# Tiles of three and of two blocks of 128 rows in an expert loop, with part of the small tiles' weight splits on GpSimd

## The chip, the cores and the metric

The kernel runs on one core of a Trainium2 chip. The metric is the device time of one execution in microseconds. Five engines work side by side, each on its own row of instructions: PE (TensorE, matmuls and transposes), DVE (VectorE), ACT (ScalarE), POOL (GpSimd) and SP (SyncE, which here only issues DMAs). An instruction starts when the one before it on its engine has been issued and the semaphores that it waits for are up.

## What is computed

Three stages follow each other on 24576 rows (8 sequences of 3072) of 256 float32 numbers. The first is a filter in the frequency domain along each sequence, the third a feed-forward network on every row. The change is in the second:

```
do_compute = x @ w_skip > 0
e_idx = argmax(x[do_compute] @ w_gate)          # one of 8 experts for each row
h = maximum(xc[mask] @ w1[e], 0.0)              # 256 -> 1024, for the rows of expert e
y[mask] = gate_w[mask, None] * (h @ w2[e])      # 1024 -> 256
out[do_compute] = xc + y
```

With the reference's inputs 12185 rows are computed. They make 13, 13, 13, 11, 12, 14, 11 and 12 blocks of 128 for the eight experts, the last block of each being filled up with padding.

## The kernel before

Every float32 operand of a matmul is split into a high and a low part, and three products are summed (high by high, high by low, low by high), since PE takes the parts at a higher rate. The high part is a copy that rounds, the low part is the operand minus the high part.

The first stage (class `Phase1`) also computes each row's expert and writes, with 192 indirect DMAs of GpSimd (L720), the list `lst` of the rows of each expert. Before the second stage, `Phase2.table` (L892 to L929) makes from the counts a table with one entry for each tile: its expert `te` and its first place in the list `tr`. A tile has TT = 384 places, three blocks of 128, so each expert's rows are rounded up to a multiple of three blocks.

`Phase2.run` (L1094 to L1119) then runs one loop over the table. Its body is a hand-made software pipeline. While tile i goes through both matmuls, the rows of tile i + 1 are gathered and turned, and its weights are loaded and split. In the order of the code one iteration does:

- `rc` is copied from `rn` on DVE (L1095): the rows of this tile, kept for the sum at the end.
- `gather` (L946): after a `hold`, three indirect DMAs of GpSimd bring the next tile's rows into `rn` (L952). A `hold` (L971) is an add of one column on GpSimd. It makes GpSimd wait, so that the DMA behind it needs no wait of its own.
- three adds of one column on GpSimd make sure that the `ob` tiles are free (L1098).
- `fetch` loads the next `w1` (1 MB, SP, L944).
- for each f of 8 slices: `up(f)` has six matmuls of 384 columns (L1018), then `hh` (ACT, L1020) and `hl` (DVE, L1021) empty PSUM. `split2(f)` splits this tile's `w2` into high (ACT, L995) and low (DVE, L996) in `w2x`.
- `tokens` loads the list's entries for a later tile into `pn` (L939), `fetch2` the next `w2` (L974).
- for each of the three blocks j: `down(j)` has eight pairs of matmuls of 512 and 256 columns (L1031, L1034). Behind `down(0)` stands `turn`, the transposes of the next tile's rows on PE (L1003) with `xh` (ACT, L1008) and `xl` (DVE, L1009). `split1` splits the next `w1` in quarters (ACT L989, DVE L990). `finish` (L1043 to L1050) adds the parts of `py` into `sb`, makes `ob` from it, holds, and scatters the rows back with one indirect DMA of GpSimd.

Each engine works through its own row in this order, so what stands later in the code waits for what stands ahead of it on the same engine. At the end of the loop all engines meet at a barrier, and GpSimd executes a drain before it.

Of the kernel before, what the change touches and what calls it, by code (L numbers as in the profile page):

```python
# [20 lines left out]
N1, N2, NT = 96, 32, 24  # L21
KP = 4 * NT + 2
NE, FE, FF = 8, 1024, 2048
TT = 384
CAP = NTOK + TT
BIG = 1 << 20
LAM = 0.01
NTB = 96
HINT = (mybir.EngineType.PE,)
# [37 lines left out]
class Flow:  # L67
# [8 lines left out]
    def __init__(self, bufs):  # L76
        self.bufs, self.steps, self.writers, self.readers = bufs, [], {}, {}
# [79 lines left out]
class Phase1:  # L157
# [385 lines left out]
    def inverse(self, b):  # L543
# [3 lines left out]
        for q in range(8):  # L547
# [16 lines left out]
            for g in (2 * q, 2 * q + 1):  # L564
# [297 lines left out]
class Keep:  # L862


    def __init__(self, nc, pool):
        self.nc = nc
        t = lambda n, shape, dt=F32: pool.tile(shape, dt, tag=n, name=n)
        self.base, self.ident = t("base", [128, NE]), t("ident", [128, 128])
        self.index, self.indexf = t("index", [32, NTB // 32, 1], I32), t("indexf", [32, NTB // 32, 1])
        self.start, self.one = t("start", [32, NE]), t("one", [32, NE])  # L870
        self.pack = t("pack", [32, 2 * NTB // 32, 32])

    def count(self):
# [4 lines left out]
    def consts(self):  # L878
        V = self.nc.vector
        V.tensor_copy(self.indexf, self.index)  # L880
        V.memset(self.one, 1.0)
        V.memset(self.pack, 0.0)
        for e in range(NE):
            V.memset(self.start[:, e : e + 1], float(TT - 1 - (e * CAP - 1 - BIG)))


class Phase2:
# [3 lines left out]

    def table(self, cp):  # L892

        nc, keep = self.nc, self.keep
        V = nc.vector
        NC = NTB // 32

        def tl(shape, tag, dt=F32):
            return cp.tile(shape, dt, tag=tag, name=tag)

        cf, nt, cum, off = (tl([32, NE], "tb" + n) for n in "abcd")
        ni = tl([32, NE], "tbi", I32)
        V.tensor_tensor(cf, keep.base[0:32, :], keep.start, op=ALU.add)
        V.tensor_copy(ni, cf)
        V.tensor_scalar(ni, ni, 7, None, op0=ALU.logical_shift_right)
        V.tensor_copy(nt, ni)
        V.tensor_scalar(nt, nt, float(-(-2048 // (TT // 128))), None, op0=ALU.mult)
        V.tensor_copy(ni, nt)
        V.tensor_scalar(ni, ni, 11, None, op0=ALU.logical_shift_right)
        V.tensor_copy(nt, ni)  # L910
        V.tensor_tensor_scan(cum, keep.one, nt, 0.0, op0=ALU.mult, op1=ALU.add)
        V.tensor_scalar(off, nt, -float(TT), float(CAP), op0=ALU.mult, op1=ALU.add)
        ge = tl([32, NC, NE], "tbg")
        over = lambda v: v.rearrange("p (o e) -> p o e", o=1).to_broadcast([32, NC, NE])
        V.tensor_tensor(ge, keep.indexf.to_broadcast([32, NC, NE]), over(cum), op=ALU.is_ge)
        ef, rf = tl([32, NC, 1], "tbx"), tl([32, NC, 1], "tby")
        V.tensor_reduce(ef, ge, axis=AX.X, op=ALU.add)
        V.tensor_tensor(ge, ge, over(off), op=ALU.mult)
        V.tensor_reduce(rf, ge[:, :, 0 : NE - 1], axis=AX.X, op=ALU.add)
        V.scalar_tensor_tensor(rf, keep.indexf, float(TT), rf, op0=ALU.mult, op1=ALU.add)  # L920
        V.tensor_scalar(keep.pack[:, 0:NC, 0:1], ef, float(NE - 1), None, op0=ALU.min)
        V.tensor_scalar(keep.pack[:, NC : 2 * NC, 0:1], rf, float(NE * CAP - TT), None, op0=ALU.min)
        turned = tl([32, 2 * NC, 32], "tbt")
        V.transpose(out=turned, in_=keep.pack)
        te = tl([1, 2 * NTB], "tbp", I32)
        V.tensor_copy(te, turned[0:1].rearrange("p c i -> p (c i)"))
        self.te, self.tr = te[:, 0:NTB], te[:, NTB : 2 * NTB]
        self.tn = tl([1, 1], "tbn", I32)
        V.tensor_copy(self.tn, cum[0:1, NE - 1 : NE])  # L929

    def reg(self, ap, lo, hi, **kw):
        return self.nc.values_load(
# [3 lines left out]
    def tokens(self, at):  # L936
        nc = self.nc
        r = self.reg(self.tr[0:1, at], 0, NE * CAP - TT, engines=[mybir.EngineType.SP])
        nc.sync.dma_start(self.pn, self.lst[ds(r, TT), :].rearrange("(p j) w -> p j w", p=128))  # L939

    def fetch(self, at):
        nc = self.nc
# [49 lines left out]
    def split2(self, f):  # L992
        nc = self.nc
        hi, lo = self.w2x[:, f, 0:256], self.w2x[:, f, 256:512]
        nc.scalar.activation(hi, self.w2r[:, f, :], AF.Copy)  # L995
        nc.vector.tensor_tensor(lo, self.w2r[:, f, :], hi.bitcast(F32), op=ALU.subtract)  # L996

    def turn(self):
        nc = self.nc
        for h in range(2):  # L1000
# [7 lines left out]
            nc.scalar.activation(self.xh[:, h, :], pt, AF.Copy)  # L1008
            nc.vector.tensor_tensor(self.xl[:, h, :], pt, self.xh[:, h, :].bitcast(F32), op=ALU.subtract)  # L1009

    def up(self, f):
        nc = self.nc
        ph = self.ps.tile([128, TT], F32, tag="ph", name="ph", bufs=4)
        k = 0
        fs = slice(f * 128, f * 128 + 128)
        for h in range(2):
            for w, x in ((self.w1h, self.xh), (self.w1h, self.xl), (self.w1l, self.xh)):
                nc.tensor.matmul(ph, w[:, h, fs], x[:, h, :], start=k == 0, stop=k == 5)  # L1018
                k += 1
        nc.scalar.activation(self.hh[:, f, :], ph, AF.Relu)  # L1020
        nc.vector.scalar_tensor_tensor(  # L1021
            self.hl[:, f, :], ph, 0.0, self.hh[:, f, :].bitcast(F32), op0=ALU.max, op1=ALU.subtract
        )

    def down(self, j):
# [34 lines left out]
    def run(self, ctx):  # L1060
        tc, nc = self.tc, self.nc
# [5 lines left out]
        t = lambda n, shape, dt=F32, pool=cr: pool.tile(shape, dt, tag=n, name=n)  # L1067
# [6 lines left out]
        t = lambda n, shape, dt=F32: cp.tile(shape, dt, tag=n, name=n)  # L1074
# [19 lines left out]
        with tc.For_i(0, n, 1, iteration_sync="reg_based", hint_engines=HINT) as it:  # L1094
            nc.vector.tensor_copy(self.rc, self.rn)  # L1095
            self.gather()
            for o in self.ob:
                nc.gpsimd.tensor_tensor(o[:, 0:1], self.dummy, self.dummy, op=ALU.add)  # L1098
            self.fetch(ds(it + 1, 1))
            for f in range(8):  # L1100
                self.up(f)
                self.split2(f)
                if f == 5:
                    nc.vector.tensor_copy(self.pc, self.pm)
                    nc.vector.tensor_copy(self.pm, self.pn)
            self.tokens(ds(it + 2, 1))
            self.fetch2()
            last = None
            for j in range(self.nj):
                py = self.down(j)  # L1110
                if j == 0:
                    self.turn()
                if last is not None:
                    self.finish(j - 1, last)
                for k in range(4 * j // self.nj, 4 * (j + 1) // self.nj):
                    self.split1(k)
                last = py
            self.finish(self.nj - 1, last)
# [204 lines left out]
```

## Time and profile before

| what | value |
|---|---|
| three runs | 3606.24, 3608.36 (median), 3610.34 us |
| the profiled execution | 3606.89 us |
| its span, first to last instruction | 3605.1 us |
| mean granted clock of PE | 0.983 |
| busy in the span | PE 97%, DVE 65%, ACT 63%, GpSimd 17% |
| the expert loop, first to last `rc` copy | 837.4 to 1448.6 us, 36 tiles |

A row of a timeline gives the start of an instruction, how long it took, its engine, line and operation, and in brackets how long the engine was idle before it and what ended that. In a stretch, the granted clock is that of PE: 1.00 is 2.4 GHz, 0.50 is 1.2 GHz. GpSimd's indirect DMAs are shown with the time in which GpSimd makes them. Their data land later.

### The profile page before, as it was taken

How to read it: one execution, taken by the hardware profiler on the slowest of the kernel's cores; microseconds unless marked ns; L12 is line 12 of the kernel's file. 1: busy time of each engine (PE TensorE's matmuls, PEld its weight loads, DVE VectorE, ACT ScalarE, POOL GpSimd, SP SyncE). 2: the span in 40 equal slices, each digit the busy share in tenths (PEclk: the TensorE clock that was granted, in tenths of full speed). 3: DMA queues.
4: the chain of work that ended last, by engine and by line, in shares of the span. 5: the costliest groups of instructions: out<-in, count | busy, mean ns of one | idle time of the engine just before them, and what ended most of it. 6: DMA issues, size and time to landing. Idle time of an engine off the chain costs nothing.

```text
span 3605.1 us, 58312 instructions
## 1 busy us (share of the span) xinstructions
PE 3484.8 (97%) x19440; PEld 3017.7 (84%) x19440; DVE 2360.1 (65%) x4284; ACT 2273.9 (63%) x4269; POOL 618.6 (17%) x718
## 2 busy tenths in 40 slices
PE   7999999977999999799999999999999999999999
PEld 7999899866999999688888888888888888888887
DVE  6999898875777777555555555555555555555554
ACT  5666576554555565466666666666666666666665
POOL 1045343454444444100000000000000000000000
PEclk8999999988999999899999999999999999999999
DMA  8888687653555555411111111111111111111100
GB/s 248 260 236 240 209 240 219 175 170 120 158 167 161 169 162 160 139 24 24 24 28 27 29 24 24 24 24 24 24 24 24 24 24 24 24 24 24 24 18 18
DMA packets 389380, 341.20 MB, mean 95 GB/s; under 512 B 246353, under 2 KB 343146, under 8 KB 389169
## 3 DMA queue, kind: packets, MB, share of 16 engines
q1 hardware_dynamic: 331296, 234.68, 24.0%
q10 hardware_dynamic: 41216, 76.56, 6.5%
q0 software_dynamic: 16656, 27.21, 2.6%
q8 instruction: 125, 2.05, 0.2%
q14 instruction: 87, 0.70, 0.1%
HBM read 214.02 MB, written 126.05 MB: 94 GB/s over the span
## 4 chain that ended last, share of the span: by engine, by line
PE 59%; DMA 0%; DVE 0%; SPq 0%; ACT 0%; DVEq 0%; issue 0%
PE ph L1178 29%; PE py L1211 29%; DMA x<-x 0%; SPq L1156 0%; DVE xt L1165 0%; ACT xh L1167 0%; DVE o L1218 0%; DVE xl L1168 0%; DVEq L1319 0%; DVEq L1165 0%
## 5 line engine op out<-in xcount | busy, mean ns | idle before, releaser
L1178 PE MATMUL ph<-xh,wi 128*128 128x512 f32 x3072 | 1075.5, 391 | 19.8 <-ACT xh L1167 19.8
L1191 DVE SCALAR_TENSOR_TENSOR e<-m,ph 128x512 f32<-128x512 f32 x768 | 526.6, 686 | 811.0 <-ACT m L1190 811.0
L1211 PE MATMUL py<-gh,wo 128*128 128x512 f32 x3072 | 828.4, 392 | 0.0
L1189 ACT ACTIVATE m<-ph 128x512 f32<-128x512 f32 x768 | 458.7, 597 | 556.9 <-PE ph L1178 556.9
L1178 PEld LDWEIGHTS ph<-xh,wi 128*128 128x128 f32 x3072 | 577.8, 188 | 153.0 <-ACT xh L1167 20.9
L1211 PEld LDWEIGHTS py<-gh,wo 128*128 128x128 f32 x3072 | 576.9, 188 | 128.4
L1178 PE MATMUL ph<-xl,wi 128*128 128x512 f32 x1536 | 606.5, 395 | 0.0
L1198 DVE TENSOR_TENSOR gl<-e,gh 128x512 fp32r<-128x512 f32 x768 | 525.4, 684 | 0.2 <-ACT gh L1197 0.2
L1190 ACT ACTIVATE m<-m 128x512 f32<-128x512 f32 x768 | 485.0, 631 | 24.4
L1211 PE MATMUL py<-gl,wo 128*128 128x512 f32 x1536 | 475.9, 391 | 0.0
L1197 ACT ACTIVATE gh<-e 128x512 fp32r<-128x512 f32 x768 | 473.0, 616 | 0.3 <-DVE e L1191 0.3
L1211 PEld LDWEIGHTS py<-gl,wo 128*128 128x128 f32 x1536 | 288.6, 188 | 61.0
L1178 PEld LDWEIGHTS ph<-xl,wi 128*128 128x128 f32 x1536 | 289.4, 188 | 58.2 <-DVE xl L1168 0.9
L1031 PE MATMUL py<-w2x,hh 128*128 128x512 f32 x864 | 306.3, 395 | 0.0
L720 POOL DMA_INDIRECT lst<-pay,ix x192 | 238.2, 1241 | 167.8 <-DVE ix L715 109.6
L1034 PE MATMUL py<-w2x,hl 128*128 128x256 f32 x864 | 241.9, 280 | 0.0
L491 PE MATMUL ps<-wh,xh 128*128 128x256 f32 x784 | 226.2, 289 | 3.0 <-ACT xh L244 2.1
L491 PE MATMUL ps<-wh,xl 128*128 128x256 f32 x784 | 223.2, 285 | 5.9 <-DVE xl L247 5.8
L491 PE MATMUL ps<-wl,xh 128*128 128x256 f32 x784 | 222.1, 283 | 0.0
L1020 ACT ACTIVATE hh<-ph 128x384 fp32r<-128x384 f32 x288 | 141.8, 492 | 90.3 <-ACT w2x L995 59.5
L1018 PE MATMUL ph<-xh,w1h 128*128 128x384 f32 x576 | 193.8, 336 | 0.7 <-DVEq L1094 0.7
L1018 PE MATMUL ph<-xl,w1h 128*128 128x384 f32 x576 | 193.6, 336 | 0.0
(179 smaller groups left out, 5450.3 us busy)
## 6 DMA issues: line engine op xcount, KB each, us to landing
w1r<-in_moe_w_dram SPq DMA_DIRECT2D x37, 1024.0 KB
w2r<-in_moe_w_dram SPq DMA_DIRECT2D x37, 1024.0 KB
ta<-av ACTq DMA_DIRECT2D x64, 392.0 KB
tr<-ct SPq DMA_DIRECT2D x64, 392.0 KB
t<-ta SPq DMA_DIRECT2D x96, 256.0 KB
ct<-cv ACTq DMA_DIRECT2D x96, 256.0 KB
x<-yv ACTq DMA_DIRECT2D x64, 384.0 KB
x<-x SPq DMA_DIRECT2D x192, 128.0 KB
```

The costliest lines, as they stand in the source:

```text
L491: nc.tensor.matmul(o[:, t, :], a[:, 2 * t + h, at : at + 128], w[:, h, ws], start=k == 0, stop=k == 11)
L720: ins = nc.gpsimd.indirect_dma_start(out=self.lst, out_offset=bass.IndirectOffsetOnAxis(ap=T(ix)[:, n : n + 1], axis=0), in_=T(pay)[:, n, ...
L1018: nc.tensor.matmul(ph, w[:, h, fs], x[:, h, :], start=k == 0, stop=k == 5)
L1031: nc.tensor.matmul(py.rearrange("p a d -> p (a d)"), self.hh[:, f, js], self.w2x[:, f, :], start=f == 0, stop=False)
L1034: nc.tensor.matmul(py[:, 0, :], self.hl[:, f, js], self.w2x[:, f, 0:256], start=False, stop=f == nf - 1)
L1178: nc.tensor.matmul(ph, w[:, h, fs], x[:, h, :], start=k == 0, stop=k == 5)
L1189: nc.scalar.activation(m, ph, AF.Relu, scale=-1.0)
L1190: nc.scalar.activation(m, m, AF.Exp, scale=-1.0)
L1191: nc.vector.scalar_tensor_tensor(e, m, 1.0, ph, op0=ALU.subtract, op1=ALU.max)
L1197: nc.scalar.activation(gh, e, AF.Copy)
L1198: nc.vector.tensor_tensor(gl, e, gh.bitcast(F32), op=ALU.subtract)
L1211: nc.tensor.matmul(py, self.wo[:, f, at : at + 128], g, start=f + k == 0, stop=f + k == 17)
```

## The change

The table now has two kinds of tiles. Of an expert's blocks as many as possible go into tiles of three, and the rest into one or two tiles of two, so that no padding block is computed beyond the last begun block. With the counts above there are 27 tiles of three, which come first, and 9 of two. Two loops run over the one table, with the same body for `nj` = 3 and 2. In tiles of two (`less`) the high parts of `w2` for f = 1, 3 and 5 move from ACT to DVE, and the low parts for f = 0 to 5 from DVE to GpSimd. A drain of GpSimd stands in each iteration. The list's entries are read as "(j p)" instead of "(p j)", so each piece read has 8 bytes instead of 24.

```diff
-        nc.sync.dma_start(self.pn, self.lst[ds(r, TT), :].rearrange("(p j) w -> p j w", p=128))
+        n = 128 * self.nj
+        nc.sync.dma_start(self.pn[:, 0 : self.nj], self.lst[ds(r, n), :].rearrange("(j p) w -> p j w", p=128))
...
     def split2(self, f):
...
-        nc.scalar.activation(hi, self.w2r[:, f, :], AF.Copy)
-        nc.vector.tensor_tensor(lo, self.w2r[:, f, :], hi.bitcast(F32), op=ALU.subtract)
+        less = self.nj < TT // 128
+        if less and f in (1, 3, 5):
+            nc.vector.tensor_copy(hi, self.w2r[:, f, :])
+        else:
+            nc.scalar.activation(hi, self.w2r[:, f, :], AF.Copy)
+        eng = nc.gpsimd if less and f < 6 else nc.vector
+        eng.tensor_tensor(lo, self.w2r[:, f, :], hi.bitcast(F32), op=ALU.subtract)
...
-        n = self.reg(self.tn[0:1, 0:1], 0, NTB - 2)
+        n, total = (self.reg(self.tn[0:1, i : i + 1], 0, NTB - 3) for i in range(2))
...
+        for first, last, self.nj in ((0, n, TT // 128), (n, total, TS // 128)):
+            with tc.For_i(first, last, 1, iteration_sync="reg_based", hint_engines=HINT) as it:
+                self.body(it)
...
+    def body(self, it):
+        nc, nj = self.nc, self.nj
+        nc.vector.tensor_copy(self.rc[:, :nj], self.rn[:, :nj])
+        self.gather()
+        for o in self.ob[:nj]:
+            nc.gpsimd.tensor_tensor(o[:, 0:1], self.dummy, self.dummy, op=ALU.add)
+        if nj == TT // 128:
+            nc.gpsimd.drain()
+        self.fetch(ds(it + 1, 1))
+        for f in range(8):
+            self.up(f)
+            self.split2(f)
...
+        if nj < TT // 128:
+            nc.gpsimd.drain()
+        self.tokens(ds(it + 2, 1))
+        self.fetch2()
```

The table itself has 17 more operations on DVE, all on 32 partitions and at most 45 columns. The rest of the diff gives `turn`, `up` and the loops over blocks the width 128 x `nj`.

GpSimd's row in the loop, before: from the hold on `rc` over the gathers to the first scatter.

```order
L971 TENSOR_TENSOR dummy<-rc,pn 128x1
L952 DMA rn<-x,pn 128x256 x3
L1098 REGISTER_ALU
L1098 TENSOR_TENSOR ob_11775<-dummy 128x1
L1098 TENSOR_TENSOR ob_11776<-dummy 128x1
L1098 TENSOR_TENSOR ob_11777<-dummy 128x1
L971 ISA
L971 TENSOR_TENSOR dummy<-ob_11775 128x1
L1050 DMA x<-ob_11775,pc 24577x256
```

The same place now in the loop of small tiles, up to the second of the six subtracts, of which the other four follow in the same way, and behind them the holds and scatters.

```order
L995 TENSOR_TENSOR dummy<-rc,pn 128x1
L976 DMA rn<-x,pn 128x256 x2
L1137 REGISTER_ALU
L1137 TENSOR_TENSOR ob_11803<-dummy 128x1
L1137 TENSOR_TENSOR ob_11804<-dummy 128x1
L1025 TENSOR_TENSOR w2x<-w2r,w2x 128x256
L1025 ISA
L1025 TENSOR_TENSOR w2x<-w2r,w2x 128x256
```

The six subtracts of `w2` have come in between the adds on `ob` and the holds of the scatters, behind the gathers.

PE's row before at the start of `down(0)`: the pairs of f = 0 to 2, with what each waits for.

```order
L1031 MATMUL py<-w2x,hh 128x512 [waits PE_I-11829_own,Activation_I-11829_own]
L1034 MATMUL py<-w2x,hl 128x256
L1031 REGISTER_ALU
L1031 MATMUL py<-w2x,hh 128x512 [waits Activation_I-11829_own]
L1034 MATMUL py<-w2x,hl 128x256
L1031 REGISTER_ALU
L1031 MATMUL py<-w2x,hh 128x512 [waits Activation_I-11829_own]
```

The same now in the loop of small tiles, again f = 0 to 2.

```order
L1063 MATMUL py<-w2x,hh 128x512 [waits Pool_I-11864_own]
L1066 MATMUL py<-w2x,hl 128x256
L1063 ISA
L1063 MATMUL py<-w2x,hh 128x512 [waits Activation_I-11864_own,Pool_I-11864_own]
L1066 MATMUL py<-w2x,hl 128x256
L1063 REGISTER_ALU
L1063 MATMUL py<-w2x,hh 128x512 [waits Pool_I-11864_own]
```

The first pairs wait for GpSimd (named Pool here), and so do those of f = 3 to 5.

DVE's row before behind `down(0)`, from the second `xl` to the first `ob`.

```order
L1009 TENSOR_TENSOR xl_11770<-pt,xh_11769 128x384
L990 REGISTER_ALU
L990 TENSOR_TENSOR w1l<-w1r,w1h 128x512
L1044 REGISTER_ALU
L1044 TENSOR_TENSOR sb<-py,sb 128x256
L1045 ISA
L1045 SCALAR_TENSOR_TENSOR ob_11775<-sb,pc,rc 128x256
```

The same place now in the loop of small tiles.

```order
L1040 TENSOR_TENSOR xl_11798<-pt,xh_11797 128x256
L1014 REGISTER_ALU
L1014 TENSOR_TENSOR w1l<-w1r,w1h 128x512
L1014 REGISTER_ALU
L1014 TENSOR_TENSOR w1l<-w1r,w1h 128x512
L1076 REGISTER_ALU
L1076 TENSOR_TENSOR sb<-py,sb 128x256
L1077 ISA
L1077 SCALAR_TENSOR_TENSOR ob_11803<-sb,pc,rc 128x256
```

Two quarters of `w1` now go with each of the two blocks, where before one went with each of the first two blocks and two with the third.

## Rows read from the trace of the kernel before

**Rows 1.** Stretch of a tile: busy us (instructions) of engines, clock, DMA share, GB/s

```profile
996.97:1014.29 17.32, 17.32 (x104) 16.33 (x103) 13.58 (x31) 10.38 (x26) 8.17 (x13) 1.00 0.49 159
```

**Rows 2.** The line of the rc copy: durations in ns, first and last start

```profile
L1095 DVE COPY rc<-rn x36: 559/561/562, 837.4 to 1448.6; 128x768 f32<-128x768 f32 x36
```

**Rows 3.** Timeline of PE: last up matmul, first of down(0), first transpose

```profile
1003.51 0.33 PE L1018 MATMUL ph<-xh,w1l 128*128 128x384 f32 x1
1003.68 0.39 PE L1031 MATMUL py<-w2x,hh 128*128 128x512 f32 x1
...
1006.46 0.27 PE L1003 MATMUL pt<-ident,rn 128*128 128x128 f32 x1
```

**Rows 4.** Timeline of DVE behind down(0) of the same tile

```profile
1007.66 1.02 DVE L1009 TENSOR_TENSOR xl<-pt,xh 128x384 fp32r<-128x384 f32 x2 [2.32 <-ACT xh L1008]
1008.61 0.68 DVE L990 TENSOR_TENSOR w1l<-w1r,w1h 128x512 fp32r<-128x512 f32 x1
1009.20 0.42 DVE L1044 TENSOR_TENSOR sb<-py,sb 128x256 f32<-128x256 f32 x1
1009.74 0.48 DVE L1045 SCALAR_TENSOR_TENSOR ob<-sb,pc,rc 128x256 f32<-128x256 f32 x1
1010.14 0.68 DVE L990 TENSOR_TENSOR w1l<-w1r,w1h 128x512 fp32r<-128x512 f32 x1
...
1013.81 0.48 DVE L1045 SCALAR_TENSOR_TENSOR ob<-sb,pc,rc 128x256 f32<-128x256 f32 x1
```

**Rows 5.** Timeline of GpSimd behind the last ob of that tile

```profile
1016.18 0.20 POOL L971 TENSOR_TENSOR dummy<-rc,pn 128x1 f32<-128x1 f32 x1
1016.54 1.26 POOL L952 DMA_INDIRECT rn<-x,pn  x1 [0.16 <-issue]
1018.11 1.27 POOL L952 DMA_INDIRECT rn<-x,pn  x1 [0.30 <-issue]
```

**Rows 6.** Groups, 850 to 1440 us: busy us, mean ns, idle before, releasers

```profile
L952 POOL DMA_INDIRECT rn<-x,pn x102 | 118.8, 1165 | 28.0 <-issue 27.7 <-DMA x<-ob,pc 0.3
...
L971 POOL TENSOR_TENSOR dummy<-ob 128x1 f32<-128x1 f32 x102 | 32.3, 317 | 243.7 <-DVE ob L1045 242.6
```

**Rows 7.** Timeline of GpSimd in the first stage: low parts by subtraction

```profile
125.18 0.85 POOL L238 TENSOR_TENSOR sl<-y,sh 128x256 fp32r<-128x256 f32 x1 [38.90 <-ACT sh L244]
...
192.27 2.40 POOL L238 TENSOR_TENSOR sl<-y,sh 128x512 fp32r<-128x512 f32 x1 [19.78 <-ACT sh L244]
...
244.43 1.30 POOL L238 TENSOR_TENSOR sl<-y,sh 128x512 fp32r<-128x512 f32 x1 [10.79 <-DVE sm L680]
...
491.35 0.74 POOL L238 TENSOR_TENSOR sl<-y,sh 128x256 fp32r<-128x256 f32 x1 [8.59 <-ACT sh L244]
```

**Rows 8.** Stretches around a fall of the clock, columns as in rows 1

```profile
755.00:760.00 5.00, 3.21 (x60) 2.07 (x58) 4.00 (x21) 1.95 (x5) 0.67 (x1) 1.00 0.74 213
...
765.00:770.00 5.00, 4.83 (x23) 4.53 (x24) 4.33 (x10) 1.97 (x4) 4.09 (x4) 0.50 1.00 350
770.00:775.00 5.00, 5.00 (x68) 4.52 (x67) 1.37 (x2) 3.70 (x8) 3.78 (x5) 0.93 0.95 273
```

**Rows 9.** Timeline at the loop's end: last scatter, first issue of the next stage

```profile
1466.94 0.99 POOL L1050 DMA_INDIRECT x<-ob,pc  x1 [0.52 <-issue]
1477.42 2.69 SPq L1156 DMA_DIRECT2D x<-x  x4
```

**Rows 10.** GpSimd's drains: shortest, median, longest in ns, first and last start

```profile
L1319 POOLq DRAIN  x5: 40/98/9961, 1466.9 to 3604.8; - x5
```

**Rows 11.** DMA issues: the scatter, median us to landing

```profile
x<-ob,pc POOLq DMA_INDIRECT x108, 2.5
```

**Rows 12.** Timelines of DVE and GpSimd ahead of the loop: table's end, last list scatter

```profile
802.73 0.13 DVE L929 CAST tbn<-tbc 1x1 int32<-1x1 f32 x1
...
824.28 0.98 POOL L720 DMA_INDIRECT lst<-pay,ix  x1 [0.30 <-issue]
```

More of the change, by code (lines that the diff above doesn't have):

```diff
@@ L23 @@
 NE, FE, FF = 8, 1024, 2048
-TT = 384
+TT, TS = 384, 256
 CAP = NTOK + TT
@@ L869, in __init__ @@
         self.index, self.indexf = t("index", [32, NTB // 32, 1], I32), t("indexf", [32, NTB // 32, 1])
-        self.start, self.one = t("start", [32, NE]), t("one", [32, NE])
+        self.start, self.one = t("start", [32, NE]), t("one", [32, 2 * NE])
+        self.rows = t("rows", [32, NE])
         self.pack = t("pack", [32, 2 * NTB // 32, 32])
@@ L884, in consts @@
             V.memset(self.start[:, e : e + 1], float(TT - 1 - (e * CAP - 1 - BIG)))
+            V.memset(self.rows[:, e : e + 1], float(e * CAP))
 class Phase2:
@@ L895, in table @@
         V = nc.vector
-        NC = NTB // 32
+        NC, NS = NTB // 32, 2 * NE
         def tl(shape, tag, dt=F32):
             return cp.tile(shape, dt, tag=tag, name=tag)
-        cf, nt, cum, off = (tl([32, NE], "tb" + n) for n in "abcd")
+        cf, nb, up, two = (tl([32, NE], "tb" + n) for n in "abcd")
         ni = tl([32, NE], "tbi", I32)
+        cnt, cum, row = (tl([32, NS], "tb" + n) for n in "efg")
         V.tensor_tensor(cf, keep.base[0:32, :], keep.start, op=ALU.add)
@@ L905, in table @@
         V.tensor_scalar(ni, ni, 7, None, op0=ALU.logical_shift_right)
-        V.tensor_copy(nt, ni)
-        V.tensor_scalar(nt, nt, float(-(-2048 // (TT // 128))), None, op0=ALU.mult)
-        V.tensor_copy(ni, nt)
+        V.tensor_copy(nb, ni)
+        V.tensor_scalar(up, nb, float(-(-2048 // (TT // 128))), None, op0=ALU.mult)
+        V.tensor_copy(ni, up)
         V.tensor_scalar(ni, ni, 11, None, op0=ALU.logical_shift_right)
-        V.tensor_copy(nt, ni)
-        V.tensor_tensor_scan(cum, keep.one, nt, 0.0, op0=ALU.mult, op1=ALU.add)
@@ L912, in table @@
[L912 to L915, printed above, removed]
+        V.tensor_copy(up, ni)
+        V.scalar_tensor_tensor(two, up, 3.0, nb, op0=ALU.mult, op1=ALU.subtract)
+        V.tensor_scalar(two, two, 2.0, None, op0=ALU.add)
+        V.tensor_scalar(nb, nb, -2.0, None, op0=ALU.add)
@@ new lines, in table @@
+        V.tensor_tensor(cnt[:, NE:NS], nb, two, op=ALU.min)
+        V.tensor_tensor(cnt[:, 0:NE], up, cnt[:, NE:NS], op=ALU.subtract)
+        V.tensor_tensor_scan(cum, keep.one, cnt, 0.0, op0=ALU.mult, op1=ALU.add)
+        V.tensor_tensor(row, cum, cnt, op=ALU.subtract)
+        V.scalar_tensor_tensor(row[:, 0:NE], row[:, 0:NE], -float(TT), keep.rows, op0=ALU.mult, op1=ALU.add)
+        V.scalar_tensor_tensor(row[:, NE:NS], row[:, NE:NS], -float(TS), keep.rows, op0=ALU.mult, op1=ALU.add)
+        V.scalar_tensor_tensor(row[:, NE:NS], cnt[:, 0:NE], float(TT), row[:, NE:NS], op0=ALU.mult, op1=ALU.add)
@@ L916, in table @@
+        step = tl([32, NS - 1], "tbs")
+        V.tensor_tensor(step, row[:, 1:NS], row[:, 0 : NS - 1], op=ALU.subtract)
+        ge, at = tl([32, NC, NS - 1], "tbg"), tl([32, NC, NS - 1], "tbh")
+        over = lambda v: v.rearrange("p (o e) -> p o e", o=1).to_broadcast([32, NC, NS - 1])
+        V.tensor_tensor(ge, keep.indexf.to_broadcast([32, NC, NS - 1]), over(cum[:, 0 : NS - 1]), op=ALU.is_ge)
         ef, rf = tl([32, NC, 1], "tbx"), tl([32, NC, 1], "tby")
+        size = tl([32, NC, 1], "tbz")
@@ L917, in table @@
         V.tensor_reduce(ef, ge, axis=AX.X, op=ALU.add)
-        V.tensor_tensor(ge, ge, over(off), op=ALU.mult)
-        V.tensor_reduce(rf, ge[:, :, 0 : NE - 1], axis=AX.X, op=ALU.add)
-        V.scalar_tensor_tensor(rf, keep.indexf, float(TT), rf, op0=ALU.mult, op1=ALU.add)
+        V.tensor_tensor(at, ge, over(step), op=ALU.mult)
+        V.tensor_reduce(rf, at, axis=AX.X, op=ALU.add)
+        small = ge[:, :, NE - 1 : NE]
+        V.tensor_scalar(size, small, float(TS - TT), float(TT), op0=ALU.mult, op1=ALU.add)
@@ L921, in table @@
+        V.tensor_tensor(size, size, keep.indexf, op=ALU.mult)
+        V.tensor_tensor(rf, size, rf, op=ALU.add)
+        V.scalar_tensor_tensor(ef, small, -float(NE), ef, op0=ALU.mult, op1=ALU.add)
         V.tensor_scalar(keep.pack[:, 0:NC, 0:1], ef, float(NE - 1), None, op0=ALU.min)
@@ L927, in table @@
         self.te, self.tr = te[:, 0:NTB], te[:, NTB : 2 * NTB]
-        self.tn = tl([1, 1], "tbn", I32)
-        V.tensor_copy(self.tn, cum[0:1, NE - 1 : NE])
+        self.tn = tl([1, 2], "tbn", I32)
+        V.tensor_copy(self.tn[:, 0:1], cum[0:1, NE - 1 : NE])
+        V.tensor_copy(self.tn[:, 1:2], cum[0:1, NS - 1 : NS])
     def reg(self, ap, lo, hi, **kw):
@@ L994, in split2 @@
         hi, lo = self.w2x[:, f, 0:256], self.w2x[:, f, 256:512]
-        nc.scalar.activation(hi, self.w2r[:, f, :], AF.Copy)
-        nc.vector.tensor_tensor(lo, self.w2r[:, f, :], hi.bitcast(F32), op=ALU.subtract)
+        less = self.nj < TT // 128
[5 more added lines that the diff above has]
+        eng.tensor_tensor(lo, self.w2r[:, f, :], hi.bitcast(F32), op=ALU.subtract)
     def turn(self):
         nc = self.nc
+        n = 128 * self.nj
         for h in range(2):
@@ L1007, in turn @@
                     self.tc.add_to_no_dep_group("turn", getattr(ins, "ins", ins))
-            nc.scalar.activation(self.xh[:, h, :], pt, AF.Copy)
-            nc.vector.tensor_tensor(self.xl[:, h, :], pt, self.xh[:, h, :].bitcast(F32), op=ALU.subtract)
+            xh, pt = self.xh[:, h, :n], pt[:, :n]
+            nc.scalar.activation(xh, pt, AF.Copy)
+            nc.vector.tensor_tensor(self.xl[:, h, :n], pt, xh.bitcast(F32), op=ALU.subtract)
     def up(self, f):
@@ L1013, in up @@
         ph = self.ps.tile([128, TT], F32, tag="ph", name="ph", bufs=4)
-        k = 0
+        k, n = 0, 128 * self.nj
         fs = slice(f * 128, f * 128 + 128)
+        ph, hh = ph[:, :n], self.hh[:, f, :n]
         for h in range(2):
             for w, x in ((self.w1h, self.xh), (self.w1h, self.xl), (self.w1l, self.xh)):
-                nc.tensor.matmul(ph, w[:, h, fs], x[:, h, :], start=k == 0, stop=k == 5)
+                nc.tensor.matmul(ph, w[:, h, fs], x[:, h, :n], start=k == 0, stop=k == 5)
                 k += 1
-        nc.scalar.activation(self.hh[:, f, :], ph, AF.Relu)
+        nc.scalar.activation(hh, ph, AF.Relu)
         nc.vector.scalar_tensor_tensor(
-            self.hl[:, f, :], ph, 0.0, self.hh[:, f, :].bitcast(F32), op0=ALU.max, op1=ALU.subtract
+            self.hl[:, f, :n], ph, 0.0, hh.bitcast(F32), op0=ALU.max, op1=ALU.subtract
         )
@@ L1093, in run @@
         self.inside = True
[L1094 to L1118, printed above, removed]
@@ L1119, in run @@
-        self.inside = False
+        for first, last, self.nj in ((0, n, TT // 128), (n, total, TS // 128)):
+            with tc.For_i(first, last, 1, iteration_sync="reg_based", hint_engines=HINT) as it:
+                self.body(it)
+        self.inside = False
+    def body(self, it):
[10 more added lines that the diff above has]
+            self.split2(f)
+            if f == 5:
+                nc.vector.tensor_copy(self.pc[:, :nj], self.pm[:, :nj])
+                nc.vector.tensor_copy(self.pm[:, :nj], self.pn[:, :nj])
+        if nj < TT // 128:
+            nc.gpsimd.drain()
+        self.tokens(ds(it + 2, 1))
+        self.fetch2()
+        last = None
+        for j in range(nj):
+            py = self.down(j)
+            if j == 0:
+                self.turn()
+            if last is not None:
+                self.finish(j - 1, last)
+            for k in range(4 * j // nj, 4 * (j + 1) // nj):
+                self.split1(k)
+            last = py
+        self.finish(nj - 1, last)
```

## The prediction

> **What bounds the kernel now.** I read first the stretches of single tiles, then the timelines of PE, DVE and GpSimd in one of them, then the stretches around the clock's falls and the loop's end. In the expert loop PE is busy for all of a tile: 17.32 of 17.32 us at full clock, with DVE at 13.6, ACT at 10.4 and GpSimd at 8.2 [rows 1]. The loop runs 36 such tiles [rows 2]. So only PE time counts there, as long as nothing else becomes longer. I call E the end of a tile's last `ob` on DVE (1013.81 + 0.48 = 1014.29 [rows 4]), and T the start of its transposes, which is where `down(0)` ends (1006.46 [rows 3]).
>
> **What the change does to the tiles.** The reference's inputs give the eight experts 13, 13, 13, 11, 12, 14, 11 and 12 blocks of 128 rows, 99 in all. Before, they fill 36 tiles of three, 108 blocks. Now 27 tiles hold three and 9 hold two. The number of tiles, and so of weight loads, is the same. What is gained must come out of the 9 small tiles.
>
> **What PE alone would say.** The up matmuls of 384 columns follow each other by 0.17 us, and a pair of down matmuls takes (1006.46 - 1003.68) / 8 = 0.348 [rows 3]. A small tile has 48 up matmuls of 256 columns (0.115 each, by columns), 16 pairs and four transposes: 5.5 + 5.6 + 0.4 = 11.5 us. Against 17.3 that is 5.8 us a tile, 52 in all. I don't think it gets them, for the following reason.
>
> **The new chain of a small tile.** In `down(0)` the first six `w2x` pairs now wait for GpSimd, and on GpSimd the six `lo` subtracts stand behind the tile's gathers. I work the period out in two pieces.
>
> From E to the next T. Nothing at the start of GpSimd's row changes: after E it does the hold of the last `ob` and its scatter, then the hold on `rc` (1016.18), then gathers from 1016.54 on, 1.57 apart [rows 5]. The second gather begins at E + 3.82 and takes 1.165 [rows 6], so it ends at E + 5.0. Two adds of one column follow, 0.2 us each as the hold is [rows 5], so the first `lo` starts about E + 5.5. Before has two subtracts of the very form 128x256 on GpSimd: 0.74 and 0.85 us [rows 7]. I take 0.78 with the step to the next one, since DVE has little to do by then; the ends are 0.74 and 0.85. Six make 4.7: the last ends at E + 10.2. PE has the pairs of f = 5, 6 and 7 left then, 3 x 0.348, so T comes at E + 11.3.
>
> From T to the next E. DVE has two `xl`, two `w1l`, `sb`, `ob`, two `w1l`, `sb`, `ob` to do in this order. In before the first `xl` starts 1.2 after T; with four transposes and 256 columns I take 0.8. Two `xl` at 0.4 each (0.48 for 384 columns, 0.95 for the two), then steps of 0.6 for a `w1l`, 0.54 from `sb` to `ob`, 0.40 from `ob` on [rows 4]: 0.8 + 0.8 + 1.2 + 0.54 + 0.40 + 1.2 + 0.54 + 0.48 = 6.0. PE's `down(1)` ends at T + 3.2, and is covered by this.
>
> The period is 11.3 + 6.0 = **17.3 us**, the same as for a tile of three. PE ends the up matmuls about E + 3.9 (they start when the third `w1l` is there, about E - 1.6), then stands still for 2.4 us and is then busy 0.35 of each 0.78. The ends of the parts (`lo` 0.74 or 0.85, first `xl` at T + 0.75 or T + 1.2) make it 16.9 to 18.2.
>
> **The clock.** PE then works for less than 2 of the 6.3 us from E + 3.9 on. In before, PE was busy for 3.21 of 5 us at 755 and then lost the full clock; the clock was 0.50 for 765 to 770 although PE worked for 4.83 of these 5 us, and came back in the next stretch [rows 8]. I therefore expect 1.2 GHz at the end of `down(0)` in most small tiles. The three last pairs then cost 1.04 more. [...] I take 1.0: period **18.3**, 8 x (18.3 - 17.3) = **+8.0 us** for the small tiles behind the first.
>
> The Trainium skill ("TensorE: Matmul & The Clock Gate", on how the gate oscillates in real kernels) says that pauses inside a loop can cost the full clock anew in every iteration. No run so far shows this inside the expert loop; by it the forecast stands as it is, and without it the full-clock rival below holds.
>
> **Between the loops.** At the end of a loop all engines meet. In before the last scatter starts at 1466.94, the next part's first transfer is issued at 1477.42 [rows 9], and between them GpSimd's drain lasts 9.96 us [rows 10]. A scatter lands after 2.5 us [rows 11], so the rest of the drain is not the scatter's. The other drains take 0.04 and 0.1 us. The long one follows 411 indirect DMAs and no other drain, which would be 24 ns for each. If that is what it pays for, then drains inside the body, each after six DMAs, cost about 0.15 us, and make the drains at the end short. The first of them, after 198 DMAs, would take 4.8. GpSimd waits 242.6 / 102 x 3 = 7.1 us in a tile for `ob` [rows 6], so none of that reaches PE. I take it so, with the other case as a rival.
>
> With a short drain a loop's end costs: scatter 1466.94 + 2.5 + 0.6 (drain's end to first issue, 1476.9 to 1477.42) and some for the last semaphores, about 1470.6, 4.5 after E. The first small tile starts with all engines empty, and PE at half clock: GpSimd needs 0.9 to the hold, 0.3, two gathers 3.0, 0.5, six `lo` 4.7, then 1.0 of pairs and 6.0 of tail, about 16.5; with 0.5 for entering the loop it ends 21.5 after E. Against one tile of three that is **+4.2**. At the end of the second loop the same short drain brings the next part forward by 1477.42 - 1470.6 = 6.8: **-6.8**.
>
> **Small parts.** The table's 17 more tiny DVE operations and the second register load lie under GpSimd's scatters into the list, which run until 825.3, while the table is done at 802.9 [rows 12]: nothing; without that cover 17 x 0.2 = 3.4 us. The token list is read in runs of 8 instead of 24 bytes: ahead of the loop the first read is on the path, I take **+0.3** (0 to 1; a whole scatter's landing is 2.5 [rows 11]). In the loop the read has most of a tile until it is used. Queued on SP behind it is the `w2r` load, which now also waits for the last `lo`, E + 10.2, and is used in the next tile, after E + 17: at most 7 us of cover. The tiles of three have the same work as before.
>
> **Sum**, against the profiled run of 3606.9: 4.2 + 8.0 - 6.8 + 0.3 = +5.7, **3612.6**, put as 3613. That run lies 1.5 below the median of the three shown, 3608.4, and inside their range of 3606.2 to 3610.3; this is part of the range given. About 0.2%, or 7.2 us, is what a measurement of this kernel can tell from no change, so 3601 to 3615.6 counts as the same.
>
> **Rivals.** (a) *The full clock holds* all through the small tiles: 3612.6 - 8.0 = 3604.6, and some 3600 with `lo` at 0.74. For it: no tile of before loses the clock. Against it: PE's pauses above. 22%.
> (b) *The `lo` subtracts are hidden*: PE paces `down(0)`, T at E + 3.9 + 2.8, then 6.0 of tail, 12.7 a tile: 8 x -4.6 = -37 and the -2.3 of the rest, about 3568. It needs GpSimd to be done by E + 4 with work that in before's timing starts at E + 5.5; hence 9%, with the cases in between.
> (c) *The drains at the loops' ends stay long*, because they pay for something other than the number of DMAs: +6.8 between the loops and no gain behind: 3612.6 + 13.6 = 3626. 13%.
> (d) *Slower, by the drain in the body*: if each takes as long as the long one, 10 us, GpSimd needs three gathers 4.7, adds 0.6, drain 10, three scatters 4.3 (each about a gather), 19.6 us for a tile of three, and 21 for a small one: 27 x 2.3 + 9 x 3.7 = +95, about 3700. It decides from a drain of some 7 us on, GpSimd's idle time. The 0.04 and 0.1 us of the other drains speak against it: 8%.
> (e) *DVE and GpSimd hold each other up*: GpSimd's 128x512 subtract took 2.40 us once and 1.30 at another time [rows 7]. For 128x256 the like would be 0.55 more. Only the first `lo` meets DVE's own two subtracts (f = 6, 7): 9 x 0.55 = +5, 3618; for all six 3642. 6%.
> The Trainium skill ("SBUF — State Buffer", on who interferes with whom) has a rule for (e): a DVE operation with two SBUF inputs and a GpSimd one that reads SBUF exclude each other for a whole instruction. The 2.40 agrees; that DVE is nearly idle while five of the six run keeps the chance low.
>
> **How the numbers follow.** Forecast 42%, 3606 to 3620 by its own ends; (a) 22, (b) 9, (c) 13, (d) 8, (e) 6. The range 3598 to 3632 leaves out (b), (d) and the bad end of (e), 19%. Faster: (b) and a quarter of (a), 15%. Slower: (c), (d), nearly all of (e) and a third of the forecast, 40%. The same: 45%.
>
> **What would show it.** In the profile of after: `py` on PE waiting for GpSimd's `w2x` some 2 us before f = 0 and 0.4 before each of the next five; a distance of 17 to 19 us between the `rc` copies of small tiles; a granted clock below 1.00 in that stretch; a drain under 1 us at both loop ends, and none that delays a scatter. A small tile of 13 us, or drains of 10, would make the prediction wrong.

## The result, and the profile after

| | before | after |
|---|---|---|
| runs (median) | 3606.24 to 3610.34 (3607.51, 4 runs) | 3639.27 to 3649.09 (3645.72, 4 runs) |
| ratio to before, 95% interval | | 1.0103 [1.0085, 1.012] |
| profiled execution, span | 3606.89, 3605.1 us | 3643.99, 3642.2 us |

The change makes the kernel 38 us slower by the medians, and 37 us by the profiled executions. The prediction was 3613 us, and 3632 at most: 33 us too low. To find the place, I follow the profiled execution stage by stage.

First, the line of the `rc` copies of after, which answers to [rows 2]. Its columns are the durations (shortest, median, longest, in ns), then the first and last start.

```profile
L1134 DVE COPY rc<-rn x36: 426/560/561, 839.4 to 1460.7; 128x768 f32<-128x768 f32 x27, 128x512 f32<-128x512 f32 x9
```

There are 27 tiles of three and 9 of two, as forecast. From first to last copy the loop takes 621.3 us, where it took 611.2. It begins 2.0 us later, which is no more than the spread of nearly one program on one chip (835.9 to 839.4 us in `c_l192`, `c_l224` and `c_l256` below).

Next, stretches of single small tiles, from one `rc` copy to the next, which answer to [rows 1]. Columns as there: the stretch, its length, the busy time (and instructions) of PE, PEld, DVE, ACT and GpSimd, then the granted clock, the DMA share and GB/s.

```profile
1334.30:1352.68 18.38, 14.80 (x86) 12.21 (x85) 10.71 (x26) 7.92 (x21) 10.26 (x16) 0.91 0.45 143
1352.68:1371.28 18.60, 16.14 (x86) 13.40 (x85) 10.79 (x27) 8.07 (x21) 10.26 (x16) 0.82 0.44 137
1371.28:1388.56 17.28, 13.74 (x86) 11.04 (x86) 10.70 (x26) 7.89 (x21) 10.21 (x16) 1.00 0.47 152
1388.56:1405.92 17.36, 13.76 (x86) 11.05 (x85) 10.71 (x27) 7.93 (x21) 10.29 (x16) 1.00 0.47 146
```

A small tile takes as long as a tile of three: 17.3 us at full clock, and 17.8 to 18.7 where the clock fell for a part of it. In the tiles at full clock PE is now idle for 3.5 us, and no engine is busy throughout. The timeline of GpSimd shows why (start, duration, line, operation, idle time before it and what ended it); it answers to [rows 5].

```profile
1353.25 1.02 POOL L1082 DMA_INDIRECT x<-ob,pc  x1 [0.56 <-issue]
...
1354.66 1.10 POOL L976 DMA_INDIRECT rn<-x,pn  x1 [0.16 <-issue]
1356.07 1.13 POOL L976 DMA_INDIRECT rn<-x,pn  x1 [0.30 <-issue]
1357.30 0.46 POOL L1137 TENSOR_TENSOR ob<-dummy 128x1 f32<-128x1 f32 x2
1357.72 4.53 POOL L1025 TENSOR_TENSOR w2x<-w2r,w2x 128x256 fp32r<-128x256 f32 x6
```

The last `ob` of the tile before ended at E = 1352.36. The six subtracts begin at E + 5.4, behind scatter, hold and gathers, and end at E + 9.9; forecast were 5.5 and 10.2. On PE's side, this is the wait that costs it most between 1320 and 1475 us (what waited, for what: us in total, times, longest).

```profile
PE py L1063 <- POOL w2x L1025: 18.5, 20, 2.0
```

At the loops' ends the long drain of [rows 10] is gone; 2.5 and 2.6 us are left. The rows are those of GpSimd's drains: in the tiles of three, in the tiles of two, and at the ends of the loops and the program.

```profile
L1139 POOLq DRAIN  x27: 3109/3432/10716, 842.3 to 1298.0; - x27
...
L1148 POOLq DRAIN  x9: 1005/4132/4197, 1324.8 to 1466.3; - x9
...
L1361 POOLq DRAIN  x7: 46/93/2569, 1311.3 to 3641.9; - x7
```

The record of a drain begins while GpSimd still works on what stands ahead of it. In the small tile shown it runs from 1358.5 to 1362.6, and the last subtract ends at 1362.25, so that only 0.4 of the 4.1 us is a wait of its own. In the tiles of three it is some 1.5 of 3.4 us, in the first iteration 7.6 of 10.7.

So far the whole is near the forecast. Now the third stage, by its first and last matmuls of one kind: before, and after.

```profile
L1178 PE MATMUL ph<-xh,wi x3072: 388/392/794, 1484.4 to 3591.8; 128*128 128x512 f32 x192
```

```profile
L1220 PE MATMUL ph<-xh,wi x3072: 390/393/796, 1489.7 to 3629.2; 128*128 128x512 f32 x192
```

It begins 5.3 us later. That is the whole difference of the first two stages; the sum of the prediction gave +5.7. But from the first to the last of these matmuls it takes 2139.5 in place of 2107.4 us. **Of the 38 us, 32 are lost in a stage in which the diff changes no instruction.** The same stretch of it, before and after, shows how:

```profile
2000.00:2439.50 439.50, 439.50 (x1922) 360.61 (x1921) 244.56 (x380) 289.88 (x501) 0.00 (x0) 1.00 0.11 25
```

```profile
2000.00:2439.50 439.50, 439.50 (x1893) 356.32 (x1892) 241.54 (x376) 286.10 (x493) 0.00 (x0) 1.00 0.11 23
```

PE is busy all the time in both, at the full granted clock, but executes 1893 matmuls instead of 1922: one takes 232.2 ns instead of 228.7. It is so throughout: 192 matmuls in a row take 43.95 us before and 44.61 to 44.63 after, in every part of the stage behind its start (counted from start to start). There are 9216 of them, and 9216 x 3.5 ns = 32 us.

### The profile page after: what moved, and what is told of

It reads as the page before. It is cut to its first block, busy times and chain, and to the rows that moved or that the text cites. A ratio compares the mean times of both kernels' runs of the same rounds, so it can differ in the third digit from the quotient of the medians.

```text
span 3642.2 us, 58047 instructions
## 1 busy us (share of the span) xinstructions
PE 3499.7 (96%) x19278; PEld 2993.3 (82%) x19278; DVE 2339.4 (64%) x4260; ACT 2256.0 (62%) x4233; POOL 633.4 (17%) x736
## 4 chain that ended last, share of the span: by engine, by line
PE 59%; DMA 0%; DVE 0%; SPq 0%; ACT 0%; DVEq 0%; issue 0%
PE ph L1220 29%; PE py L1253 29%; DMA x<-x 0%; SPq L1198 0%; DVE xt L1207 0%; ACT xh L1209 0%; DVE o L1260 0%; DVE xl L1210 0%; DVEq L1361 0%; DVEq L1207 0%
## 5 line engine op out<-in xcount | busy, mean ns | idle before, releaser
L1220 PE MATMUL ph<-xh,wi 128*128 128x512 f32 x3072 | 1089.4, 395 | 14.0 <-ACT xh L1209 14.0
L1253 PE MATMUL py<-gh,wo 128*128 128x512 f32 x3072 | 838.4, 395 | 0.0
L1063 PE MATMUL py<-w2x,hh 128*128 128x512 f32 x792 | 297.6, 414 | 19.3 <-POOL w2x L1025 18.5
L1066 PE MATMUL py<-w2x,hl 128*128 128x256 f32 x792 | 225.8, 285 | 0.0
L1063 PEld LDWEIGHTS py<-w2x,hh 128*128 128x128 f32 x792 | 152.7, 193 | 62.5 <-POOL w2x L1025 32.6
L1050 PE MATMUL ph<-xh,w1h 128*128 128x384 f32 (+1 forms) x576 | 188.8, 328 | 9.3 <-issue 7.3
L1052 ACT ACTIVATE hh<-ph 128x384 fp32r<-128x384 f32 (+1 forms) x288 | 133.8, 465 | 101.5 <-PE ph L1050 53.4
```

The source lines that it names most:

```text
L1050: nc.tensor.matmul(ph, w[:, h, fs], x[:, h, :n], start=k == 0, stop=k == 5)
L1063: nc.tensor.matmul(py.rearrange("p a d -> p (a d)"), self.hh[:, f, js], self.w2x[:, f, :], start=f == 0, stop=False)
L1066: nc.tensor.matmul(py[:, 0, :], self.hl[:, f, js], self.w2x[:, f, 0:256], start=False, stop=f == nf - 1)
L1253: nc.tensor.matmul(py, self.wo[:, f, at : at + 128], g, start=f + k == 0, stop=f + k == 17)
```

## The experiments

What does the change do to the third stage, if not its instructions? It adds two small constants, `rows` and a wider `one`, to the tiles that live through all stages (`Keep`): 64 bytes in each partition. All SBUF tiles that are allocated after them from the left, among them the operands that PE streams in the third stage (`xh`, `xl`, `gh`, `gl`), lie 64 bytes higher for that. The weights that it holds (`wi`, `wo`) are allocated from the right and stay. Theory A is that this shift slows the matmuls; rival B that the program's place or length does it; rival C that it is the chip.

The experiments ran on four chips. On three of them the first two stages took longer in every trace (first `rc` copy at 887 to 899 us, on the fourth at 836 to 839), and the whole times of before were longer too (3695, 3764 and 3713 us, on the fourth 3607). So whole times are compared on one chip alone; the third stage, at one and the same placement, took the same time on all.

**The shift alone** (`a_pad64`):

```diff
+        self.pad = t("pad", [128, 16])
         self.pack = t("pack", [32, 2 * NTB // 32, 32])
...
+        V.memset(self.pad[:, 0:1], 0.0)
```

> The kernel before with one unused tile of 64 bytes per partition among the tiles that live through all stages, so that every left-hand SBUF tile of the second and third stage lies 64 bytes higher, as in the changed kernel. The instructions are otherwise the same. Theory A (the third stage's matmuls got slower, 43.95 to 44.62 us for 192, since the tiles that they read moved by 64 bytes): 44.6 us for 192 matmuls there, and about 3639 us in all. Rival B (the new instructions ahead of the third stage, their number or place in memory, slow it): 43.95 and 3607 us. Rival C (the chip or the day): 43.95 here, or the same shift in the kernel before of this call.

The kernel before, with nothing but this padding and one memset of a column of it:

```profile
2000.00:2439.50 439.50, 439.50 (x1893) 356.36 (x1892) 240.58 (x374) 285.98 (x492) 0.00 (x0) 1.00 0.11 25
```

1893 matmuls, 44.62 us for 192: the number of after. Theory A holds for the third stage, and B is out: no instruction of a loop was touched. The whole kernel took 1.0055 [1.0035, 1.0075] of before, 18 us more and not the 32 expected. The third stage takes its 32 us; the rest must lie in the first two, which vary on this chip. The expert loop, from the first to the last `rc` copy, took 629.5 us here, and 639.5 in `d_drain` on the same chip. What makes that difference isn't shown.

**The change without the shift** (`b_same`): the constants lie in unused columns of `pack`.

```diff
-        self.start, self.one = t("start", [32, NE]), t("one", [32, 2 * NE])
-        self.rows = t("rows", [32, NE])
+        self.start, self.spare = t("start", [32, NE]), t("spare", [32, NE])
         self.pack = t("pack", [32, 2 * NTB // 32, 32])
+        self.one = self.pack[:, 0, 8 : 8 + 2 * NE]
+        self.rows = self.pack[:, 1, 8 : 8 + NE]
```

> The changed kernel with its two new small constants kept in unused columns of a tile that was there already, so that the tiles of the third stage lie where they lay before. All instructions of the loops stay. Theory A: 43.95 us for 192 matmuls of the third stage, and 3612 to 3614 us, +5 against before. Rivals B and C: 44.6 and 3644 us.

```profile
2000.00:2439.50 439.50, 439.50 (x1922) 360.61 (x1921) 244.55 (x380) 289.58 (x502) 0.00 (x0) 1.00 0.11 25
```

The third stage is back at 1922 matmuls, 43.95 us for 192, on the same chip as `a_pad64`, so rival C is out too. The ratio is 0.9981 [0.9965, 0.9996], so not slower than before, and a little better than the +5 us expected. On this chip a tile of three takes 17.7 to 18.6 us in place of 17.32, and a small one 17.4 to 18.4, so that a small tile costs no more than the one that it replaces. So the change as it was meant is worth nothing that matters, and the 1% loss is the 64 bytes.

**The splits back from GpSimd** (`c_dve`), on top of `b_same`:

```diff
-        less = self.nj < TT // 128
+        less = False
```

> As the kernel with the addresses of before, and the splits of the small tiles all as in the tiles of three (high parts on ACT, low parts on DVE, none on GpSimd). Theory (GpSimd's subtracts behind the gathers set the period of small tiles): DVE's low part of f = 7 is done about 8 us after the end of the last ob, T follows 0.4 later, and with 6.0 of tail the period falls from 18.1 to about 14.5 us, with the clock at 1.00: -29 us for eight tiles, about 3585 with the addresses of before. Rival (the period is set by the tail, or by PE's clock, or the small tile is bound by DVE all the same): 17 us or more, 3605 to 3613.

The ratio is 0.9881 [0.9857, 0.9905], 41 us less than before on this chip, where 22 were expected. On the chip where before takes 3607 us, `c_l256` below, the same program at the same distance, takes 31 us less. Seven of the eight periods between the small tiles' `rc` copies are 14.0 us. A stretch of one, and PE's waits from 1416 to 1515 us:

```profile
1474.40:1488.40 14.00, 12.82 (x87) 11.16 (x86) 11.06 (x29) 8.67 (x25) 5.83 (x10) 1.00 0.58 187
```

```profile
PE ph L1052 <- DVE w1l L1016: 5.3, 8, 0.7
PE py L1065 <- DVE w2x L1027: 2.4, 7, 0.3
```

The clock stays at 1.00, and PE waits some 1 us a tile. The edit also gives three high parts from DVE back to ACT; that it was the six subtracts, behind the gathers on GpSimd, that held the small tile at 17.3 us is what PE's waits for GpSimd in after say. With their pauses gone, the clock no longer falls. DVE, which GpSimd was to relieve, does the same work within a shorter tile. A version with the subtracts ahead of the gathers wasn't run.

**The drain alone** (`d_drain`), in the kernel before:

```diff
             for o in self.ob:
                 nc.gpsimd.tensor_tensor(o[:, 0:1], self.dummy, self.dummy, op=ALU.add)
+            nc.gpsimd.drain()
```

> The kernel before with one GpSimd drain in each iteration, behind the adds on ob, as in the changed kernel's tiles of three; nothing else. Theory (the drain at the loop's end pays for every indirect DMA since the last drain): drains of 3 to 4 us in the loop, one of about 10 in the first iteration, period 17.32 as before, and at the end about 2.6 us in place of 9.96, so the third stage starts 7 us earlier: about 3600. Rival (the long drain is a fixed cost of leaving the loop): 9.96 at the end all the same, 3607.

GpSimd's drains in the loop, and at its end:

```profile
L1099 POOLq DRAIN  x36: 3317/3608/10461, 901.8 to 1542.8; - x36
...
L1320 POOLq DRAIN  x5: 46/93/2552, 1556.5 to 3688.1; - x5
```

2.55 us are left of the 9.96 at the loop's end, and the third stage's first matmul comes 29.2 us after the last `rc` copy, where it takes 35.5 in `a_pad64` on the same chip: 6.4 us gained. The one whole time, 3690 us, lies within the runs of before there (3683 to 3705). The long drain comes from what stands before it, and is not the price of leaving a loop. Its length doesn't follow the number of DMAs, though: 10.5 us behind 198 of them, 9.96 behind 411 in before.

**What in the shift counts.** Four paddings of the kernel before tell apart whether the place of the streamed tiles counts or their distance to the weights. Padding on the right (behind `wo`) moves the weights 64 bytes down.

```diff
         self.wo = cp.tile([128, 16, 512], F32R, tag="wo", name="wo")
+        self.pad = cp.tile([128, 16], F32, tag="pad3", name="pad3")
```

`e_right64`, the right alone:

> The kernel before with 64 unused bytes on the right-hand side of SBUF: the third stage's weights (the tiles that PE loads as stationary) lie 64 bytes lower, the tiles that it streams stay. In the kernel before weights begin at byte 96 of a row of 128 and streamed tiles at byte 32; in the changed kernel both at 96. Here both begin at 32. Theory A1 (what counts is how the two lie to each other): 44.6 us for 192 matmuls. Theory A2 (what counts is where the streamed tiles lie): 43.95.

```profile
2000.00:2439.50 439.50, 439.50 (x1893) 356.35 (x1892) 240.01 (x373) 286.64 (x494) 0.00 (x0) 1.00 0.11 25
```

44.62 us for 192. The streamed tiles lie where they lay in before, and the matmuls are as slow as in after: the distance counts, A1.

`f_both64`, right and left:

> The kernel before with both paddings: streamed tiles 64 bytes higher (byte 96 of 128), weights 64 lower (byte 32). Theory A1: 64 apart again, 43.95 us for 192 matmuls. Theory A2: 44.6.

44.80 us for 192. Neither theory had this: A1 expected 43.95, as if the pattern repeated after 128 bytes. `g_pad32` is `a_pad64` with 32 bytes, `h_pad128` with 128.

> The kernel before with streamed tiles 32 bytes higher, at byte 64 of 128, weights at 96 as before, 32 apart. Theory A1: a time between or like one of the two, 43.95 to 44.62. Theory A2 with a limit at 64 bytes: 43.95 or less, since the tile now begins at a multiple of 64.

> The kernel before with streamed tiles 128 bytes higher, so at byte 32 of 128 as before. Both theories, if the pattern repeats after 128 bytes: 43.95 us for 192 matmuls. If it repeats after 256 or more: not 43.95.

Both: 44.80 us for 192, as in `f_both64`. A2 is out, with its 43.95 for `g_pad32`; the 44.80 is more than A1 gave it, too. Since `h_pad128` has the same distance as `f_both64`, by another pair of places, and the same time, and neither equals before, A1 stands, with a reach of more than 128 bytes.

The whole times of these four were single runs of 3721, 3744, 3731 and 3751 us. All lie below the one run of before beside them, 3764 us, though their third stage takes 31 to 41 us more than before's 2112.9. So their first two stages must have been faster than before's there by more than the padding costs; no trace of before on this chip shows how. Only the third stage itself is compared here.

`c_l192`, `c_l224` and `c_l256` are `c_dve` with 192, 224 and 256 bytes of padding on the left.

> The kernel without GpSimd splits, with the streamed tiles of the third stage 192 bytes higher than in the kernel before. What is tested is the law of the distance. So far 192 matmuls took 43.95 us at a distance (start of the streamed tiles minus start of the weights, taken to 256) of 64 bytes, 44.62 at 128 (reached in two ways), 44.80 at 96 and at 192 (the latter reached in two ways). Here it is 0. If the same start is a clash, 45 us or more; if small distances are good, 43.95 or less. The small tiles keep their period of 14.0 us.

> The same with 224 bytes, a distance of 32. If small distances are good: 43.95 or less; if only 64 is a good one: 44.6 to 44.8.

> The same with 256 bytes, a distance of 64 again as before. If the law repeats after 256 bytes: 43.95 us for 192 matmuls. If the distance counts over a longer reach: another value.

The same stretch in `c_l192` and in `c_l224`:

```profile
2000.00:2439.50 439.50, 439.50 (x1941) 364.04 (x1940) 247.73 (x386) 291.41 (x506) 0.00 (x0) 1.00 0.13 25
```

```profile
2000.00:2439.50 439.50, 439.50 (x1886) 353.03 (x1885) 240.34 (x375) 285.34 (x491) 0.00 (x0) 1.00 0.10 25
```

No guess gave a rule: 0 is no clash but the best place, as "small distances are good" had it, and 32, by the same guess a good one, is among the worst. 256 bytes of padding give the time of none again. All together, with the distance from the start of the weights to the start of the streamed tiles, taken to 256 bytes:

| distance | kernels | 192 matmuls | third stage, first to last matmul |
|---|---|---|---|
| 0 | c_l192, best | 43.52 us | 2092.2, 2091.7 us |
| 32 | c_l224 | 44.80 | 2154.0 |
| 64 | before, b_same, c_dve, d_drain, c_l256 | 43.95 | 2112.0 to 2113.4 |
| 96 | g_pad32 | 44.80 | 2154.1 |
| 128 | after, a_pad64, e_right64 | 44.62 | 2144.4 to 2145.4 |
| 192 | f_both64, h_pad128 | 44.80 | 2153.6, 2153.7 |

13 kernels on several chips fall into four times, by this one number. Only 128 and 192 were reached by two pairs of places; for 0, 32 and 96 the weights lay at one place alone. What in the chip makes it so isn't shown by any run here: why 0 is best, and why 128 is better than 96, stays open, and so do the distances 160 and 224.

In single runs on one chip, beside 3606.95 us of before, `c_l192` took 3557.55, `c_l256` 3575.75 and `c_l224` 3616.67. The same program with the same small tiles is thus 10 us slower or 49 us faster than before, by 32 bytes of an unused tile.

**The version that beats both** (`best`) is `c_l192` again, timed.

> The same program as c_l192 (tiles of three and two, no GpSimd splits, distance 0), timed against the kernel before. From the one look: 3557.6 against 3606.9, a ratio of 0.986. On a chip where the first two stages run slower, the same gain of some 50 us: 0.985 to 0.989.

3617.67 against 3712.85 us of before on the same chip, a ratio of 0.9756 [0.9732, 0.978]. That is 95 us, where some 50 were expected. The first stage of `best` was slow on this chip (first `rc` copy at 897.0 us), but its tiles of three take 17.2 to 17.6 us, where those of `d_drain` on another slow chip took 17.3 to 18.6. Before left no trace here, so where the other 45 us come from isn't shown. On the chip where before takes 3607 us a single run gave 0.986.

## Why the prediction was wrong

By its steps:

- **The small tile**: forecast 17.3 us at full clock from E to E, found 17.29 and 17.35 in the two tiles that kept it. The two pieces hold too: in these tiles T comes 11.06 and 11.13 us after E (forecast 11.3), and the next E 6.2 after T (6.0); in the tile shown `lo` runs from E + 5.4 to 9.9 (5.5 to 10.2). The reasoning that GpSimd's row, not PE, sets the period was right, and `c_dve` shows it by taking the subtracts away (14.0 us; 14.5 was expected).
- **The clock**: I took +1.0 us for each of the eight tiles behind the first, a size that no run had shown. From E to E they take 18.38, 18.60, 17.29, 17.35, 18.40, 17.75, 18.66 and 18.16 us. Where the clock fell it cost 0.4 to 1.4 us, on average the 1.0, most of it ahead of T (11.5 to 12.1 us from E). But two of the eight tiles went without a fall. The term is +6.2 in place of +8.0.
- **Between the loops**: forecast 21.5 us from the E of the last tile of three to that of the first small one, found 23.44 (1310.53 to 1333.97). The term is +6.1 in place of +4.2.
- **The drains**: right in what they do to the loop's end, wrong in their length inside the loop. I had 0.15 us from 24 ns for each DMA, and 4.8 in the first iteration; as waits of their own they take about 1.5, 0.4 and 7.6 us. GpSimd's 7.1 us of waiting cover the usual ones, as said, so they cost nothing: the period of tiles of three is 17.32 as in [rows 1], and the first one 21.27 where before had 21.26. From the last E to the first matmul of the third stage it is 11.2 us after 18.3: -7.1 (forecast -6.8).
- **The sum up to the third stage**: +5.7 forecast, +5.3 found. Much of the agreement is luck. The terms for the clock and for the time between the loops miss by -1.8 and +1.9 and cancel. The loop began 2.0 us later, and three tiles of before (17.5, 18.5 and 17.9 us) took 2.0 more than the others, which after's tiles of three did not.
- **The step that failed**: the sum ends at the start of the third stage and puts that stage's own time at no change, without a term or a reason. The small parts count the table's new operations as time alone, "under GpSimd's scatters into the list [...]: nothing". As time this is right: there are 13 more of them by the trace (33 after 20) and not 17, and they are done at 806.1 us, ahead of the last scatter into the list at 826.8. But the table's new constants also take 64 bytes of SBUF for the whole kernel, and that moves the operands of a stage with 59% of the chain. None of the rivals looks behind the loop's end. The runs showed +32 us there, of the +38: 44.62 us for 192 matmuls after 43.95, with the 64 bytes alone (`a_pad64`), and 43.95 again without them (`b_same`).

Rivals (a) to (e) were about the second stage. (a) came true in two tiles of eight. (b), (c) and (d) didn't happen. (e) came true in part. The first two subtracts on GpSimd take 0.72 and 0.73 us and the last two 0.73, but the third and the fourth 0.91, and these two overlap with DVE's own two subtracts of `w2` (f = 6 and 7), which are slower as well. GpSimd's third, then DVE's two:

```profile
1359.10 0.91 POOL L1025 TENSOR_TENSOR w2x<-w2r,w2x 128x256 fp32r<-128x256 f32 x1
```

```profile
1358.72 0.70 DVE L1025 TENSOR_TENSOR w2x<-w2r,w2x 128x256 fp32r<-128x256 f32 x1
...
1359.68 0.61 DVE L1025 TENSOR_TENSOR w2x<-w2r,w2x 128x256 fp32r<-128x256 f32 x1
```

In before DVE's subtract of this form takes 425 ns on average:

```profile
L996 DVE TENSOR_TENSOR w2x<-w2r,w2x 128x256 fp32r<-128x256 f32 x272 | 115.6, 425 | 0.0
```

The rule of the Trainium skill ("SBUF — State Buffer", on who interferes with whom) fits that, since both sides take longer. The price is 0.4 us a tile on GpSimd's row, so that the six take 4.53 us together, less than the 4.7 of the forecast.

## What to carry to other kernels

Before a kernel's diff is costed, list what it allocates, and what is allocated after that: a shift of 32 or 64 bytes can change the pace of matmuls in a stage that nobody touched. When a profile shows a busy PE at full clock, compare the number of matmuls in an equal stretch, since the busy share cannot show a slower pace; and when the pace differs, try paddings of 32 to 256 bytes, which cost only that space. Before work is moved to relieve a busy engine, look at what it is queued behind on the engine that takes it: here six subtracts of 0.76 us, put behind two gathers, made a tile of 14 us one of 17 to 18.

## What the runs showed of the hardware

- The time of a matmul of 512 float32r columns, in an unbroken row of them with a weight load for each, went with the distance of streamed and stationary operand in SBUF, taken to 256 bytes, in 13 kernels: from 226.4 ns (439.5 us for 1941) to 233.2 (1885), all at a granted clock of 1.00. In the third stage that is 62 us between best and worst.
- The record of a GpSimd drain behind its indirect DMAs is 3.1 to 4.2 us long in most iterations of after, and 10.7 in the first one, behind 198 of them; 0.4 to 2.1 and 7.6 us of that come after GpSimd's last work ahead of it. With a drain in each iteration the one at the loop's end takes 2.6 us instead of 9.96.
- A subtract of two SBUF operands of 128x256 took 0.70 and 0.61 us on DVE while GpSimd ran the like (425 ns on average in before), and 0.91 on GpSimd while DVE ran it (0.72 to 0.73 otherwise).
- The Trainium skill ("TensorE: Matmul & The Clock Gate", on how the gate oscillates in real kernels) says that pauses in a loop can cost the full clock in each iteration. The trace agrees in six of the eight small tiles behind the first, where the granted clock is 0.82 to 0.91 and the tile takes 0.4 to 1.4 us more, but not in all: in two of them PE had much the same idle time (3.5 us) and kept 1.00.
